# Decoding float64 weights beside an attention that TensorE bounds: the steps of a group gathered in one unit, a clamp on GpSimd, and the hash behind the values

## The chip, the core and the metric

The kernel runs on one core of a Trainium2 chip. The core has five engines that work side by side, each through its own queue in order: TensorE (PE; its weight loads are PEld), VectorE (DVE), ScalarE (ACT), GpSimd (POOL) and SyncE (SP), which here only issues transfers (DMA). The metric is device time in microseconds (us) of the whole program. Before the change it is 759.25 us, the median of three runs (758.73 to 759.68).

## The reference

Attention in which a query sees only the keys with the same six-bit hash, and behind it a feed-forward network with a convolution over the sequence and a gate. Four batches, 8 heads, 768 positions, head size 64; model width 512, inner width 1024, three taps.

```python
q_bits = (np.einsum('bhsd,dk->bhsk', q, proj) > 0).astype(np.int64)
k_bits = (np.einsum('bhsd,dk->bhsk', k, proj) > 0).astype(np.int64)
...
mask = q_bucket[:, :, :, None] == k_bucket[:, :, None, :]
scores = scale * np.matmul(q, k.transpose(0, 1, 3, 2))
scores = np.where(mask, scores, -1000000000.0)
scores = scores - np.max(scores, axis=-1, keepdims=True)
attn = np.exp(scores)
attn = attn / (np.sum(attn, axis=-1, keepdims=True) + 1e-09)
return np.matmul(attn, v).astype(np.float32)
...
h = np.maximum(x @ w_in, 0.0)
...
for k in range(K):
    conv_out += conv_w[k][None, None, :] * hp[:, k:k + S, :]
gate = 1.0 / (1.0 + np.exp(-conv_out))
return (h * gate @ w_out).astype(np.float32)
```

The weights w_in, w_out and conv_w come as float64.

## The kernel before

**Pairs and units.** Two heads of a batch form a pair: 16 pairs. A unit is 128 queries of one head of a pair; a pair has 12 units, in the order of its query blocks of 256 and, within a block, head 0 then head 1 with two units each. The outer loop runs over i = 0 to 194; k is the number of the unit within its pair (i = 12 x pair + k). Unit i issues: on TensorE its products (L253: four matmuls into one score buffer of PSUM, hash bits included as extra rows of K2 and Q2); on VectorE its maximum (L266), which also moves the scores to SBUF as tile e, and a small scaled copy of it (L270); the transposes of unit i - 3 (L296) on TensorE and their copy to SBUF, tile at (L303), on ScalarE; its exponential on ScalarE (L273). In the first six pairs the division by the sum is done behind the values: sums and their reciprocals (L287, L288) on VectorE, spread by GpSimd (rec, L290) and two transposes (L317); in the later pairs GpSimd divides e itself (L281).

**The values.** Every fourth unit (i = 7, 11, 15 and so on, AVS) issues the 24 matmuls of the values of one query block (L322). In the next unit ScalarE evicts (`high`: rs, L327, or xh, L336), and in the unit after that VectorE and GpSimd finish (`low`: x, L331, then xh and xl on GpSimd, L332 and L333, or xl, L339). [...]

**One ring of score buffers.** Scores, transposes and hashes take their PSUM tiles by turns from a ring of three ("S"). In program order products and transposes alternate, so each waits for the reader of the third before it: the transposes issued in unit i for VectorE's maximum of unit i - 1, and the products of unit i for ScalarE's copy of the transposes issued in unit i - 2. A hash takes a turn of its own.

**The next pair.** During a pair, `prepare` makes the operands of the next one out of its loaded Q and K (tile R, one buffer) in seven steps, one a unit: GpSimd rounds the high part (hi, L171), TensorE computes the hash (L186), VectorE makes bits of it (L189), GpSimd scales them (L191) and takes the low part (R, L176); SP sends every part to its rows (L174, L195, L178). It begins at k = 3 in the first pair, k = 2 in the second and k = 1 in the others (PREP). Six units later SP loads the next v and R (L165, L158); R's load must wait until the last low part (k<-R) has landed.

**The weights.** 16 blocks of 128 x 512 float64 numbers come as pairs of int32 words (rawi, rawo), one block loaded every four units (`fetch`, i = 2, 6, 10 and so on). A block takes nine steps: ScalarE's Abs of the upper word (L87, tile wl); VectorE's zero test (L89), shift and mask (L91), joining (L93), mask (L95) and lower part (L97); ScalarE's rounding (L105); GpSimd's subtraction and addition (L107, L109). `background` is called once a unit and moves each block that is under way on by a step (one or two instructions), each in another unit; a new block begins about every 4.1 units (RATE).

**The feed-forward** of a batch runs two pairs after its attention: 16 rounds of hidden (L360) and output (L390), with Relu, gate and taps on the other engines (L365 to L379). The first one stands behind unit 74.

The program order of each engine is the order in which this Python code issues; nothing reorders it.

Of the kernel before, what the change touches and what calls it, by code (L numbers as in the profile page):

```python
# [7 lines left out]
F32 = mybir.dt.float32  # L8
F32R = mybir.dt.float32r
# [24 lines left out]
AVS = (1 + NCK, 0, 0, 0)  # L34
PREP = (3, 2, 1)
PREP_N = 6
W0 = 6
RATE = 4.1
HRATE = 2.5
WC = 512  # L40
# [3 lines left out]
def lsh_attention_conv_ffn(ctx, tc, qk, v, hw, w_in, conv_w, w_out, consts, ident_in, out):  # L44
# [28 lines left out]

    def decode(raw, n, name):

        pr = raw.rearrange("p (n two) -> p n two", two=2)
        lo, hi = pr[:, :, 0].bitcast(U32), pr[:, :, 1].bitcast(F32)
        up, low = (ring(wp, bufs, [P, WC], I32, f"w{x}", f"w{x}{name}")[:, :n]
                   for x, bufs in (("u", 3), ("l", 3)))
        upf, lowf = up.bitcast(F32), low.bitcast(F32)
        V = nc.vector
        nc.scalar.activation(lowf, hi, AF.Abs)  # L87
        yield 2
        V.scalar_tensor_tensor(upf, lowf, F64_MIN, hi, ALU.is_ge, ALU.mult)  # L89
        yield 1  # L90
        V.tensor_scalar(low, up, 3, 0x3FFFFFFF, ALU.logical_shift_left, ALU.bitwise_and)  # L91
        yield 0
        V.scalar_tensor_tensor(up, up, -0x40000000, low, ALU.bitwise_and, ALU.bitwise_or)  # L93
        yield 2
        V.tensor_scalar(low, up, -0x800000, None, ALU.bitwise_and)  # L95
        yield 0
        V.scalar_tensor_tensor(lowf, lo, 2.0 ** -52, lowf, ALU.mult, ALU.mult)  # L97
        return upf, lowf

    def split_weight(raw, name):  # L100

        up, low = yield from decode(raw, WC, name)
        yield 2
        blk = weights[name] = cp.tile([P, 2, WC], F32R, tag=f"w{name}", name=f"w{name}")
        nc.scalar.copy(blk[:, 0, :], up)  # L105
        yield 2
        nc.gpsimd.tensor_tensor(up, up, blk[:, 0, :].bitcast(F32), ALU.subtract)  # L107
        yield 1
        nc.gpsimd.tensor_tensor(blk[:, 1, :], up, low, ALU.add)  # L109

    def decode_taps(raw):
        up, low = yield from decode(raw, NFC * 3, "cw")
        nc.vector.tensor_tensor(cw.rearrange("p f k -> p (f k)"), up, low, ALU.add)

# [13 lines left out]

    def background(rate, stop):

        step[0] += 1
        if rate and fetched and step[0] // rate > (step[0] - 1) // rate:
            splits.append(split_weight(*fetched.pop(0)))
        now = splits[:]
        while now:
            for g in now[:]:
                ended = next(g, None)
                if ended is None:
                    splits.remove(g)
                if ended is None or ended >= stop:  # L140
                    now.remove(g)

# [261 lines left out]
    def ffn(b, xs, fill, last):  # L404
# [4 lines left out]
        for i in range(len(todo) + FLAG):  # L409
            if i < len(todo):  # L410
                run.append(hidden(b, *todo[i], xs))
                next(run[i])
            if 1 <= i <= len(todo):
                next(run[i - 1], None)
            if i == 0:
                fill()
            fetch(1)
            background(HRATE, 2)
# [10 lines left out]
            background(HRATE, 2)  # L429

# [15 lines left out]
    for i in range(n + LAG):  # L446
# [15 lines left out]
        if u:
# [37 lines left out]
        if w and w.tq == QB // P - 1 and w.h == 1:  # L500
# [61 lines left out]
```

## Time and profile before

| | |
|---|---|
| Median of three runs | 759.25 us |
| Profiled execution: its own time | 758.92 us |
| Its span in the profile | 757.1 us |
| Granted TensorE clock | 0.99 |
| Attention with decode, feed-forward of batch 0 | to about 210, to about 282 us |

```profile
PE   5989989888889999999999999999999999999997
DVE  7778979778757646566657665666656665554653
...
PEclk8999999999999999999999999999999999999999
```

These lines cut the span in 40 slices of about 19 us and give the busy share of each in tenths. A row of the chain of waits has start, duration, engine and line; a row of a timeline has the tile that is written, the one read, and in brackets the idle time of the engine before it and what ended that. A row of groups has the count, the busy time in us and the mean of one in ns, then idle time. In the windows, each engine's busy time in us stands in the order PE, PEld, DVE, ACT, POOL, then clock, DMA share and GB/s.

### The profile page before, as it was taken

How to read it: one execution, taken by the hardware profiler on the slowest of the kernel's cores; microseconds unless marked ns; L12 is line 12 of the kernel's file. 1: busy time of each engine (PE TensorE's matmuls, PEld its weight loads, DVE VectorE, ACT ScalarE, POOL GpSimd, SP SyncE). 2: the span in 40 equal slices, each digit the busy share in tenths (PEclk: the TensorE clock that was granted, in tenths of full speed). 3: DMA queues.
4: the chain of work that ended last, by engine and by line, in shares of the span. 5: the costliest groups of instructions: out<-in, count | busy, mean ns of one | idle time of the engine just before them, and what ended most of it. 6: DMA issues, size and time to landing. Idle time of an engine off the chain costs nothing.

```text
span 757.1 us, 13345 instructions
## 1 busy us (share of the span) xinstructions
PE 717.0 (95%) x4588; PEld 586.6 (77%) x4588; DVE 498.0 (66%) x1212; ACT 511.9 (68%) x954; POOL 358.1 (47%) x355
## 2 busy tenths in 40 slices
PE   5989989888889999999999999999999999999997
PEld 3867767666679887777779988777779998778986
DVE  7778979778757646566657665666656665554653
ACT  5867777776755558778775547778775556875554
POOL 4345856565555324655735323556653433441222
PEclk8999999999999999999999999999999999999999
DMA  4656486482622103365541302256461211000011
GB/s 139 158 175 199 112 203 172 121 232 67 158 50 63 63 1 105 75 166 153 126 119 34 95 1 104 50 149 154 111 159 40 63 43 62 3 1 1 0 43 42
DMA packets 30355, 72.16 MB, mean 95 GB/s; under 512 B 5936, under 2 KB 7504, under 8 KB 30288
## 3 DMA queue, kind: packets, MB, share of 16 engines
q1 hardware_dynamic: 30000, 71.27, 34.8%
q8 instruction: 36, 0.59, 0.3%
q14 instruction: 31, 0.25, 0.1%
q10 hardware_dynamic: 288, 0.05, 0.0%
HBM read 27.40 MB, written 6.29 MB: 45 GB/s over the span
## 4 chain that ended last, share of the span: by engine, by line
PE 77%; DVE 15%; ACT 2%; DMA 2%; POOL 2%; issue 1%; DVEq 0%; SPq 0%; POOLq 0%; ACTq 0%
PE o L390 18%; PE h L360 17%; PE v L322 15%; PE s L253 13%; PE t L296 13%; DVE e L266 6%; DMA R<-in_qk 2%; PE hash L186 1%; DVE wuo L93 1%; DVE wlo L97 1%; DVE wui L93 1%; DVE st L270 1%; ACT e L273 1%; DVE wli L97 1%; DVE x L331 1%
## 5 line engine op out<-in xcount | busy, mean ns | idle before, releaser
L266 DVE TENSOR_SCALAR_CACHE_REDUCE e<-s 128x768 f32<-128x768 f32 x192 | 183.0, 953 | 87.3 <-PE s L253 80.8
L273 ACT ACTIVATE e<-e,st 128x768 f32<-128x768 f32 x192 | 180.7, 941 | 28.5 <-DVE st L270 13.9
L303 ACT COPY at<-t 128x768 f32<-128x768 f32 x192 | 152.0, 792 | 62.7 <-PE t L296 62.7
L296 PE MATMUL t<-ident,e 128*128 128x128 f32 x1152 | 162.6, 278 | 16.6 <-DVE e L266 14.0
L281 POOL TENSOR_SCALAR e<-e,st 128x768 f32<-128x768 f32 x120 | 109.2, 910 | 126.1 <-ACT at L303 65.0
L296 PEld LDWEIGHTS t<-ident,e 128*128 128x128 f32 x1152 | 130.9, 142 | 43.4 <-DVE e L266 23.7
L369 DVE SCALAR_TENSOR_TENSOR ht<-ht,cw 128x384 f32<-128x384 f32 (+1 forms) x128 | 113.1, 883 | 72.5 <-ACT ht L367 70.3
L379 POOL TENSOR_TENSOR g<-ht,g 128x384 fp32r<-128x384 f32 x64 | 72.9, 1138 | 169.3 <-ACT g L378 137.3
L390 PE MATMUL o<-wo,g 128*128 128x512 f32 x576 | 143.0, 394 | 1.0 <-POOL g L379 1.0
L360 PE MATMUL h<-xh,wi 128*128 128x386 f32 x512 | 142.2, 341 | 1.3 <-ACT ht L365 1.3
L322 PE MATMUL v<-at,v 128*64 128x256 f32 x1152 | 138.1, 385 | 0.0
L390 PEld LDWEIGHTS o<-wo,g 128*128 128x128 f32 x576 | 107.2, 188 | 22.0 <-POOL g L379 1.4
L253 PE MATMUL s<-K,Q 128*128 128x384 f32 x384 | 116.2, 384 | 3.9 <-DVE e L266 2.7
L322 PEld LDWEIGHTS v<-at,v 128*64 128x64 f32 x1152 | 83.2, 138 | 41.6 <-issue 9.2
L253 PE MATMUL s<-k,q 96*128 96x384 f32 x384 | 99.6, 340 | 2.5 <-DVE e L266 2.2
L360 PEld LDWEIGHTS h<-xh,wi 128*128 128x128 f32 x512 | 94.1, 188 | 5.3 <-ACT ht L365 1.8
L372 ACT ACTIVATE ht<-ht 128x384 f32<-128x384 f32 x64 | 33.6, 526 | 90.2 <-DVE ht L369 90.2
L360 PE MATMUL h<-xl,wi 128*128 128x386 f32 x256 | 86.8, 339 | 0.0
L253 PEld LDWEIGHTS s<-K,Q 128*128 128x128 f32 x384 | 58.5, 191 | 33.5 <-issue 18.6
L253 PEld LDWEIGHTS s<-k,q 96*128 96x128 f32 x384 | 70.6, 191 | 3.6 <-ACT q L233 3.1
L373 DVE TENSOR_TENSOR ht<-ht 128x384 f32<-128x384 f32 x64 | 43.1, 674 | 33.9 <-ACT ht L372 33.9
L176 POOL TENSOR_TENSOR R<-R,hi 128x768 fp32r<-128x768 f32 x30 | 59.2, 1973 | 0.2
(75 smaller groups left out, 613.5 us busy)
## 6 DMA issues: line engine op xcount, KB each, us to landing
R<-in_qk SPq DMA_DIRECT2D x15, 768.0 KB
K<-hi SPq DMA_DIRECT2D x60, 192.0 KB
v<-in_v SPq DMA_DIRECT2D x16, 384.0 KB
out<-osb SPq DMA_DIRECT2D x24, 256.0 KB
Q<-hi SPq DMA_DIRECT2D x30, 192.0 KB
q<-hi SPq DMA_DIRECT2D x30, 192.0 KB
Q<-R SPq DMA_DIRECT2D x30, 192.0 KB
k<-R SPq DMA_DIRECT2D x30, 192.0 KB
```

The source lines that it names most:

```text
L176: nc.gpsimd.tensor_tensor(lo, R, hi.bitcast(F32), ALU.subtract)
L253: nc.tensor.matmul(self.sp[:, half, :HS], A[:, h, qs], C[:, h, half * HS:(half + 1) * HS], start=(kk == 0), stop=(kk == 1))
L266: nc.vector.tensor_scalar(self.e.rearrange("p (a b) -> p a b", a=2), self.sp[:, :, :HS], MASKED, None, ALU.max, ALU.max, accum_out=self.st ...
L273: nc.scalar.activation(self.e, self.e, AF.Exp, bias=self.st[:, 1:2], scale=SCALE, accum_out=self.sum)
L281: nc.gpsimd.tensor_scalar(self.e, self.e, self.st[:, 3:4], 0.0, ALU.mult, ALU.add)
L296: nc.tensor.transpose(self.tp[:, c // 3, c % 3 * P:(c % 3 + 1) * P], self.e[:, c * P:(c + 1) * P], ident)
L303: nc.scalar.copy(pr.at[self.h][:, :, :, self.tq * P:(self.tq + 1) * P], self.tp[:, :, :3 * P].rearrange("p j (c q) -> p j c q", c=3))
L322: nc.tensor.matmul(av[h * D:(h + 1) * D, :QB], vt[:, c, h, :], ats[h][:, c // 3, c % 3, :], start=(c == 0), stop=(c == NCK - 1), tile_posi ...
L360: nc.tensor.matmul(hp[:, :HW], w, x[:, c0:c0 + HW], start=(n == 0), stop=(n == 3 * NCC - 1))
L369: nc.vector.scalar_tensor_tensor(t[:, a:z], ht[:, o + k - 1 + a:o + k - 1 + z], cw[:, f, k:k + 1], t[:, a:z], ALU.mult, ALU.add)
L379: nc.gpsimd.tensor_tensor(g[:, 1, :], t, g[:, 0, :].bitcast(F32), ALU.subtract)
L390: nc.tensor.matmul(op, l, r, start=(f == 0 and n == 0), stop=(f == NFC - 1 and n == 2))
```

## The change

- A block's decode is now `Decode`: `size` (ScalarE's Abs), `clamp` (GpSimd: minimum and maximum against two constants, in place), `upper` (VectorE: shift and mask of the clamped size, then joining with the raw upper word) and `lower` (VectorE, as before). The zero test L89 is gone: four VectorE steps instead of five.
- All blocks are one chain, `split_weights`. A block's size is issued one block ahead; its clamp is issued in the middle of the block before it, behind the subtraction and addition (`ends`) of the block before that.
- `background(3.75)` is called only in the units that issue values (`burst`, i = 7, 11 and so on) and issues three or four VectorE steps there, in front of the next unit's maximum; the feed-forward calls it twice a round with one step. The taps get their own generator, a step a unit.
- The values' `low` half waits for the next such unit; before, it came two units after the values.
- `prepare` begins at k = 3 in every pair: its hash stands directly behind the values' matmuls on TensorE, and each of its steps and transfers, with the loads of v and R, comes one or two units later than before from the second pair on.

The core of the diff:

```diff
-PREP = (3, 2, 1)
+PREP = 3
...
-W0 = 6
-RATE = 4.1
-HRATE = 2.5
+W0 = 7
+RATE = 3.75
...
+        def size(self):
+            nc.scalar.activation(self.lowf, self.hi.bitcast(F32), AF.Abs)
+        def clamp(self):
+            nc.gpsimd.tensor_scalar(self.lowf, self.lowf, F32_MAX, F64_MIN, ALU.min, ALU.max)
+        def upper(self):
+            V, up, low = nc.vector, self.up, self.low
+            V.tensor_scalar(low, low, 3, 0x3FFFFFFF, ALU.logical_shift_left, ALU.bitwise_and)
+            yield
+            V.scalar_tensor_tensor(up, self.hi, -0x40000000, low, ALU.bitwise_and, ALU.bitwise_or)
+            yield
...
+        while fetched:
+            raw, name = fetched.pop(0)
+            nxt = None
+            if fetched:
+                nxt = Decode(fetched[0][0], WC, fetched[0][1])
+                nxt.size()
+            yield from d.upper()
+            if ends:
+                ends()
+            if nxt:
+                nxt.clamp()
+            yield from d.lower()
+            blk = weights[name] = cp.tile([P, 2, WC], F32R, tag=f"w{name}", name=f"w{name}")
+            nc.scalar.copy(blk[:, 0, :], d.upf)
+            def ends(d=d, blk=blk):
+                nc.gpsimd.tensor_tensor(d.upf, d.upf, blk[:, 0, :].bitcast(F32), ALU.subtract)
+                nc.gpsimd.tensor_tensor(blk[:, 1, :], d.upf, d.lowf, ALU.add)
+            d = nxt
...
-    def background(rate, stop):
+    def background(n):
+        due[0] += n
+        while due[0] >= 1:
+            due[0] -= 1
+            next(weights_todo, None)
...
-        done, outs, lows = lows, [], outs
-        for high, low in lows:
+        burst = AVS[(i - LAG) % 4] > 0
+        for high, low in outs:
             high()
+        lows, outs = lows + outs, []
...
-        for high, low in done:
-            low()
+        if burst:
+            for high, low in lows:
+                low()
+            lows = []
...
+        if burst and i >= W0:
+            background(RATE)
-        if u and k == PREP[min(pi, 2)] and pi + 1 < len(pairs):
+        if u and k == PREP and pi + 1 < len(pairs):
             prep[0] = pairs[pi + 1].prepare()
```

VectorE's queue from the unit at i = 18 to the one at i = 20, before. The names carry batch, pair or chunk and a number; e and st belong to a unit (e_1_3_1 is pair 1, tile 3, head 1, i = 19, a values unit), wui and wli to a block of w_in.

```order
L270 TENSOR_SCALAR st_1_2_1_635<-st_1_2_1_635 128x1
L89 SCALAR_TENSOR_TENSOR wui_0_627<-wli_0_628,rawi_0_397 128x512
L266 TENSOR_SCALAR e_1_3_1_668,st_1_3_1_667<-s_1_3_1_662 128x768
L270 TENSOR_SCALAR st_1_3_1_667<-st_1_3_1_667 128x1
L91 TENSOR_SCALAR wli_0_628<-wui_0_627 128x512
L93 SCALAR_TENSOR_TENSOR wui_0_627<-wui_0_627,wli_0_628 128x512
L266 TENSOR_SCALAR e_1_4_0_707,st_1_4_0_705<-s_1_4_0_700 128x768
L270 TENSOR_SCALAR st_1_4_0_705<-st_1_4_0_705 128x1
L95 TENSOR_SCALAR wli_0_628<-wui_0_627 128x512
L97 SCALAR_TENSOR_TENSOR wli_0_628<-rawi_0_397,wli_0_628 128x512
```

And the same units after:

```order
L298 TENSOR_SCALAR st_1_2_1_636<-st_1_2_1_636 128x1
L294 TENSOR_SCALAR e_1_3_1_661,st_1_3_1_660<-s_1_3_1_655 128x768
L298 TENSOR_SCALAR st_1_3_1_660<-st_1_3_1_660 128x1
L359 TENSOR_TENSOR x_0_2_675<-v_0_2_512,rs_0_2_513 128x256
L96 SCALAR_TENSOR_TENSOR wui_0_446<-rawi_0_398,wli_0_447 128x512
L101 TENSOR_SCALAR wli_0_447<-wui_0_446 128x512
L103 SCALAR_TENSOR_TENSOR wli_0_447<-rawi_0_398,wli_0_447 128x512
L94 TENSOR_SCALAR wli_0_561<-wli_0_561 128x512
L294 TENSOR_SCALAR e_1_4_0_719,st_1_4_0_717<-s_1_4_0_712 128x768
```

x, three steps of one block and the first step of the next (wli_0_561) now all stand between the two maxima of i = 19 and i = 20.

GpSimd's queue at the same place, before (R_2 and hi_2 are the next pair's, xh and xl the finished values):

```order
L290 TENSOR_SCALAR rec_1_1_1_610<-sums_1_0_0_445 128x256
L332 TENSOR_SCALAR xh_0_277<-x_0_2_621 128x256
L333 TENSOR_TENSOR xl_0_278<-x_0_2_621,xh_0_277 128x256
L171 TENSOR_SCALAR hi_2_1_648<-R_2_372 128x768
L107 TENSOR_TENSOR wui_0_488<-wui_0_488,wi_0_625 128x512
L109 TENSOR_TENSOR wi_0_625<-wui_0_488,wli_0_489 128x512
```

and after:

```order
L318 TENSOR_SCALAR rec_1_1_1_617<-sums_1_0_0_457 128x256
L204 TENSOR_TENSOR R_2_375<-R_2_375,hi_2_0_564 128x768
L360 TENSOR_SCALAR xh_0_274<-x_0_2_675 128x256
L361 TENSOR_TENSOR xl_0_275<-x_0_2_675,xh_0_274 128x256
L133 TENSOR_TENSOR wui_0_316<-wui_0_316,wi_0_558 128x512
L134 TENSOR_TENSOR wi_0_558<-wui_0_316,wli_0_317 128x512
L89 TENSOR_SCALAR wli_0_561<-wli_0_561 128x512
L199 TENSOR_SCALAR hi_2_1_705<-R_2_375 128x768
```

The clamp of wli_0_561 (L89 of the changed kernel), on which VectorE's last step of the burst waits, stands behind xh, xl, subtraction and addition.

ScalarE's queue from i = 7 to i = 9, before (at is the copy of transposes, rs the values' factors):

```order
L273 ACTIVATE e_0_3_1_287,sums_0_2_0_204<-e_0_3_1_287,st_0_3_1_286 128x768
L327 COPY rs_0_0_280<-v_0_0_279 128x256
L303 COPY at_0_1_0_297<-t_0_3_0_332 128x6x128
L273 ACTIVATE e_0_4_0_329,sums_0_4_0_328<-e_0_4_0_329,st_0_4_0_327 128x768
L303 COPY at_0_1_1_298<-t_0_2_1_354 128x6x128
L273 ACTIVATE e_0_5_0_347,sums_0_4_0_328<-e_0_5_0_347,st_0_5_0_346 128x768
L87 ACTIVATE wli_0_377<-rawi_0_160 128x512
```

and after:

```order
L301 ACTIVATE e_0_3_1_284,sums_0_2_0_204<-e_0_3_1_284,st_0_3_1_283 128x768
L86 ACTIVATE wli_0_313<-rawi_0_160 128x512
L86 ACTIVATE wli_0_317<-rawi_0_272 128x512
L355 COPY rs_0_0_277<-v_0_0_276 128x256
L331 COPY at_0_1_0_294<-t_0_3_0_338 128x6x128
L301 ACTIVATE e_0_4_0_335,sums_0_4_0_334<-e_0_4_0_335,st_0_4_0_333 128x768
```

Two sizes now stand in front of the factors and of the copy, that of the first block (rawi_0_160) and that of the second (rawi_0_272). On SP the load of rawi_0_272 stands, before and after, fourteen transfers behind that of rawi_0_160: behind the first high part (four transfers), the bits (eight) and the first low part (two) of the next pair.

More of the change, by code (lines that the diff above doesn't have):

```diff
@@ L72, in lsh_attention_conv_ffn @@
     nc.vector.memset(zero[64:96], 0.0)
[L74 to L109, printed above, removed]
-    def decode_taps(raw):
-        up, low = yield from decode(raw, NFC * 3, "cw")
-        nc.vector.tensor_tensor(cw.rearrange("p f k -> p (f k)"), up, low, ALU.add)
+    class Decode:
+        def __init__(self, raw, n, name):
+            pr = raw.rearrange("p (n two) -> p n two", two=2)
+            self.lo, self.hi = pr[:, :, 0].bitcast(U32), pr[:, :, 1]
+            self.up, self.low = (ring(wp, 3, [P, WC], I32, f"w{x}", f"w{x}{name}")[:, :n] for x in "ul")
+            self.upf, self.lowf = self.up.bitcast(F32), self.low.bitcast(F32)
+        def size(self):
[8 more added lines that the diff above has]
+            yield
+        def lower(self):
+            V, up, low = nc.vector, self.up, self.low
+            V.tensor_scalar(low, up, -0x800000, None, ALU.bitwise_and)
+            yield
+            V.scalar_tensor_tensor(self.lowf, self.lo, 2.0 ** -52, self.lowf, ALU.mult, ALU.mult)
+            yield
@@ new lines, in split_weights @@
+    def split_weights():
+        d = Decode(fetched[0][0], WC, fetched[0][1])
+        d.size()
+        yield
+        d.clamp()
+        yield
+        ends = None
+        while fetched:
[16 more added lines that the diff above has]
+            d = nxt
+        ends()
@@ L116, in lsh_attention_conv_ffn @@
+    def decode_taps(raw):
+        d = Decode(raw, NFC * 3, "cw")
+        d.size()
+        yield
+        d.clamp()
+        yield
+        yield from d.upper()
+        yield from d.lower()
+        nc.vector.tensor_tensor(cw.rearrange("p f k -> p (f k)"), d.upf, d.lowf, ALU.add)
     blocks = [(w_in[c * P:(c + 1) * P, 2 * n * WC:2 * (n + 1) * WC], f"i{c}_{n}")
@@ L118, in lsh_attention_conv_ffn @@
     blocks += [(w_out[f * P:(f + 1) * P], f"o{f}") for f in range(NFC)]
-    fetched, splits, step = [], [], [0]
+    fetched, due, taps = [], [0], []
+    weights_todo = split_weights()
     def fetch(n):
@@ L127, in fetch @@
         del blocks[:n]
-    def background(rate, stop):
[L131 to L141, printed above, removed]
+    def background(n):
[3 more added lines that the diff above has]
+            next(weights_todo, None)
     class Pair:
@@ L477, in lsh_attention_conv_ffn @@
             next(first, None)
-        for high, low in done:
-            low()
+        if burst:
+            for high, low in lows:
+                low()
+            lows = []
         for _ in range(1 + NCK if ending else AVS[(i - LAG) % 4]):
@@ L494, in lsh_attention_conv_ffn @@
         if i == 3:
-            splits.append(decode_taps(cwr))
-        if i >= W0 - 4:
+            taps.append(decode_taps(cwr))
+        for g in taps:
+            next(g, None)
+        if i >= W0 - 5:
             fetch(i % 4 == 2)
-        if i >= 1:
-            background(RATE if i >= W0 else 0, 1)
         if w and w.tq == QB // P - 1 and w.h == 1:
```

11 lines of the change are left out of this document (5 added, 6 removed).

## The prediction

> **What bounds the kernel now.** First the page, then the stretches that it suggests.
>
> ```profile
> PE 717.0 (95%) x4588; PEld 586.6 (77%) x4588; DVE 498.0 (66%) x1212; ACT 511.9 (68%) x954; POOL 358.1 (47%) x355
> ...
> 48.09:190.12 142.03, 124.91 (x892) 96.66 (x894) 119.24 (x263) 105.78 (x193) 86.10 (x87) 0.99 0.59 158
> 291.66:380.69 89.03, 89.03 (x666) 68.73 (x668) 55.36 (x214) 70.03 (x131) 53.66 (x56) 1.00 0.47 117
> ```
>
> TensorE is busy for 95% of the span. The view of windows splits that: in the early stretch, where the weights are decoded, 124.9 of 142.0 us; in the late one, where attention stands alone, 89.0 of 89.0. Only early can this change win; late it can only lose. The chain of waits gives the length of a group of four units, from one values matmul to the next.
>
> ```profile
> 24.67 2.74 PE v L322 x24
> ...
> 48.09 3.07 PE v L322 x24
> ...
> 190.12 2.74 PE v L322 x24
> ...
> 291.66 2.76 PE v L322 x24
> 300.31 2.74 PE v L322 x24
> ...
> L317 PE MATMUL v<-ident,rec 128*128 128x128 f32 x36 | 7.4, 289 | 0.0
> ```
>
> Late, a group is 300.31 - 291.66 = 8.65 us, all TensorE. Early pairs add the transposes of the factors (7.4 us / 18 groups = 0.41): a floor of **9.05**, and 0.85 more in a group with a hash (row below). The values units are i = 7, 11, ..., 71; I call them V1 to V17. V1 starts at 24.67, V3 at 48.09, V16 at 190.12. Between V1 and V16 lie 15 groups, five with a hash: floor 15 x 9.05 + 5 x 0.85 = 140.0, measured 165.45, so **25.4 us over the floor**. The view of waits says where:
>
> ```profile
> PE t L296 <- DVE e L266: 14.0, 17, 1.4
> PE s L253 <- DVE e L266: 4.9, 5, 2.2
> PE hash L186 <- DMA R<-in_qk: 3.2, 2, 2.8
> PE hash L186 <- ACT wi L105: 3.0, 1, 3.0
> ```
>
> 18.9 us wait for VectorE's maxima, which stand in its queue behind decode steps; 6.2 us wait in front of a hash. (The last row names ScalarE; I take it for R's load as well, since a hash reads nothing that ScalarE's L105 writes.) Both kinds are what the change touches.
>
> **The change part by part.** *Removed.* One VectorE step per block, L89, goes:
>
> ```profile
> L89 DVE SCALAR_TENSOR_TENSOR wui<-wli,rawi x8: 695/1174/1618, 32.9 to 111.3; 128x512 f32<-128x512 f32 x8
> L97 DVE SCALAR_TENSOR_TENSOR wli<-rawi,wli x8: 692/693/693, 38.9 to 117.6; 128x512 f32<-128x512 uint32 x8
> L91 DVE TENSOR_SCALAR wlo<-wuo x8: 416/418/560, 123.8 to 205.6; 128x512 int32<-128x512 int32 x8
> ```
>
> That is 16 x about 1.2 us of VectorE time. The four that stay cost 0.42 (a shift or mask, L91) or 0.69 us (L97; L93 and the new form on the raw words are taken at the same) when nothing disturbs them: 2.2 us a block. The durations above those come from GpSimd:
>
> ```profile
> 47.30 1.27 POOL L109 TENSOR_TENSOR wi<-wui,wli 128x512 fp32r<-128x512 f32 x1
> ...
> 47.86 0.99 DVE L91 TENSOR_SCALAR wli<-wui 128x512 int32<-128x512 int32 x1
> ...
> 48.53 2.01 POOL L176 TENSOR_TENSOR R<-R,hi 128x768 fp32r<-128x768 f32 x1
> 48.89 2.20 DVE L93 SCALAR_TENSOR_TENSOR wui<-wui,wli 128x512 int32<-128x512 int32 x1
> ```
>
> L91 ends 0.28 after L109 does, L93 0.55 after L176: a decode step that meets a GpSimd step waits for its end and then runs; GpSimd's next step is held in turn (L176 began at 48.53, while L91 ran to 48.85). They alternate. For the place of a maximum:
>
> ```profile
> 51.09 0.62 PE L253 MATMUL s<-K,Q 128*128 128x384 f32 x2
> ...
> 52.10 0.96 DVE L266 TENSOR_SCALAR_CACHE_REDUCE e<-s 128x768 f32<-128x768 f32 x1 [1.01 <-PE s L253]
> ```
>
> *Moved: the burst.* All decode steps of a group (four, and three in every fourth group) now stand in the values unit between its maximum and the next. Let its products start at 0. A plain unit takes (8.65 - 2.74) / 4 = 1.48 on TensorE, half of it products. So after this unit (1.48), the factors (0.41), the values (2.74), the next unit (1.48) and products (0.74) it is at a transpose at 6.85, or 7.2 with values of 3.07 as at 48.09; I take 7.0. That transpose needs the score buffer that the next unit's maximum frees. VectorE begins the first maximum at 1.0 (51.09 to 52.10) and is through with it, its small step and x (some 0.45 together) at 2.4. From there it alternates with GpSimd's xh (0.41), xl (0.73), then subtraction and addition of an earlier block (1.27 for the addition above, and I take the subtraction at the same).
> - Four steps, clamp ready (V6 to V8, V10 to V12): 0.42 to 2.85, xh to 3.2, 0.69 to 3.8, xl to 4.5, 0.28 to 4.75, subtraction to 6.0, 0.55 to 6.55; the maximum ends at 7.55. TensorE waits **0.5**.
> - Three steps (V5, V9, V13), and V1, V2 with no earlier block: nothing.
> - The fourth kind (V3, V4, V14 to V17): a block's first step stands in the burst in which its clamp is issued, and that clamp stands on GpSimd behind xh, xl, subtraction and addition. Addition ends at 7.4, clamp 8.1, step 8.5, maximum 9.5: **2.5** each.
>
> *Added: the clamp.* No row shows it.
>
> ```profile
> L281 POOL TENSOR_SCALAR e<-e,st 128x768 f32<-128x768 f32 x120 | 109.2, 910 | 126.1 <-ACT at L303 65.0 <-DVE st L280 54.4 <-PE hash L186 3.8
> L332 POOL TENSOR_SCALAR xh<-x 128x256 fp32r<-128x256 f32 x18 | 8.3, 459 | 6.0 <-DVE x L331 6.0
> ```
>
> By columns between 256 (0.46) and 768 (0.91), 512 are **0.68**. Bounds: 0.46, and 1.27 (the two-input addition of as many): over six bursts -1.3 to +3.5 us. The Trainium skill, GPSIMD Engine Reference, "4.1 Engine selection", prefers VectorE for elementwise work but calls one-input steps on GpSimd roughly line-rate; by its 1.2 GHz 512 columns would be some 0.43 (an estimate), which would take 1.5 us from the sum. The rows show 768 in 0.91, slower than that, and I go by them.
>
> *Moved: ScalarE's first step.* The size (Abs) of the following block is now issued one block ahead, on ScalarE in front of the values' eviction and the next copy of transposes. In V1 to V4 that block's load was asked for only one unit earlier, and it stands on SP behind the next pair's Q and K transfers.
>
> ```profile
> 20.86 0.86 SPq L195 DMA_DIRECT2D k<-bits  x1
> ...
> 27.01 0.71 SPq L195 DMA_DIRECT2D q<-bits  x1
> ...
> 29.04 0.58 SPq L125 DMA_DIRECT2D rawi<-in_w_in  x1
> ...
> 30.08 0.59 PE L253 MATMUL s<-K,Q 128*128 128x384 f32 x2
> ...
> 35.84 0.60 SPq L178 DMA_DIRECT2D k<-R  x1
> ...
> 39.93 0.38 SPq L158 DMA_DIRECT2D R<-in_qk  x1
> 40.36 0.47 SPq L125 DMA_DIRECT2D rawi<-in_w_in  x1
> ...
> 42.21 0.66 ACT L87 ACTIVATE wli<-rawi 128x512 f32<-128x512 f32 x1
> ...
> 44.21 0.85 PE L186 MATMUL hash<-R,hw_sb 128*32 128x384 f32 x8 [2.79 <-DMA R<-in_qk]
> ...
> 45.21 0.62 DVE L189 TENSOR_SCALAR bits<-hash,cst 128x384 fp32r<-128x384 f32 x1 [2.88 <-DMA rawi<-in_w_in]
> ...
> 47.70 0.80 ACT L303 COPY at<-t 128x768 f32<-128x768 f32 x1 [3.22 <-PE t L296]
> ...
> 51.21 0.37 ACT L327 COPY rs<-v 128x256 f32<-128x256 f32 x1 [1.79 <-PE v L322]
> ```
>
> The load issued at 40.36 is the event nearest to 45.21: 4.85 us to land. The second block, issued at 29.04, would land at 33.9; then Abs 0.66, rs 0.37, the copy at 0.80: 35.7, and only then can TensorE run the products that started at 30.08. **V1 loses 5.6.** Its lost time hides the next one: the last part of K still lands some 4.1 after its issue (35.84 to 39.93), R follows, the third block lands at 44.4, ScalarE is through at 46.2 where the shifted schedule asks at 44.8: **1.4** more in V2. In exchange the wait for R at 44.21 falls inside. So V3 comes at about 49.5, 6.7 over the floor in two groups, where 48.09 is 5.3 over. V4 loses another **2.6**: its load stands on SP behind the pair's parts from V3. GpSimd has the first at 8.8 after V3's products (clamp and 0.8), four transfers of some 0.6 end at 11.2, the eight of the hash (20.86 to 27.72: 6.9) at 18.1, two more at 19.2; landed at 23.3 (4.1, no R ahead), ScalarE through at 25.1 (1.83), asked at 12.4 + 10.1 = 22.5. Later blocks are asked for five units or more ahead.
>
> *Moved: the hash* goes behind the values in all pairs. Its R has landed by then: the 6.2 us go, nothing else is late in their place there. But the pair's last K part now comes two units later (k = 9, not 7).
>
> ```profile
> 323.58 0.90 SPq L178 DMA_DIRECT2D k<-R  x1
> ...
> 327.78 0.39 SPq L158 DMA_DIRECT2D R<-in_qk  x1
> 333.58 0.61 PE L253 MATMUL s<-K,Q 128*128 128x384 f32 x2
> ```
>
> R's load is held until that part has landed, so 327.78 is its landing, 4.2 after issue; its first reader starts at 333.58, 0.85 sooner without the hash ahead of it. k = 7 to k = 9 takes a values unit and a plain one, 2.74 + 2 x (8.65 - 2.74) / 4 = 5.7. The margin of 5.8 shrinks to about nothing: I take 0.15 for each of some ten pairs, **+1.5**, with bounds of 0 and, at a landing of 5.2, 10.
>
> *x's step one values unit later*: it is in no one's way; its buffers have two groups.
>
> **Sum.** After, V1 to V16: 6.7 (V1, V2) + 2.5 x 4 (V3, V4, V14, V15) + 2.6 + 0.5 x 6 = 22.3 over the floor, before 25.4: -3.1. From V16 to the feed-forward: twice 2.5 = 5.0, and no decode is left in front of the last exponential; before, TensorE is idle there for 34.9 - 29.5 = 5.4 (row below): -0.4. K late: +1.5. Together **-2.0 us**, on the profiled 758.92 (span 757.1 and 1.8 around it), which lies 0.3 below the median of 759.25; on the median: **757.2**.
>
> ```profile
> 190.10:225.00 34.90, 29.50 (x205) 23.41 (x204) 24.23 (x50) 22.61 (x43) 19.44 (x20) 1.00 0.44 105
> ```
>
>
> **The rivals.**
> - *Faster.* The alternation is looser than I drew it: xl, subtraction and addition come when the burst is over, decode runs at 0.42 and 0.69, clamps end at about 6.8. Then the 0.5 vanish (-3.0) and each of the six 2.5 becomes 1.3 (-7.2): **747**. For it: half of L93's rows before are undisturbed. Against: there GpSimd had other units to work in. The Trainium skill, SBUF — State Buffer, "Who interferes with whom", has the port pair of VectorE and GpSimd locked for a whole instruction; the rows above agree, and by that rule this rival fails.
> - *No change.* K's last part lands late in every pair, 0.4 on average: +4 instead of +1.5: **759.7**. Early, a V4-like stretch gives it slack; late there is none.
> - *Slower.* ScalarE behind weights that have not landed. My price uses 4.85 from issue to landing. V8, V11 and V14 ask just as their block lands, by the chain hash, twelve transfers on SP, load. From about 5 us on, V1, V2, V4, V8, V11 and V14 each lose what is over; 6.5 us costs 6 x 1.65 = 10 us: **767**. For it: the load goes out amid Q and K transfers. Against: later, TensorE's own delays give ScalarE slack.
>
> **How the numbers follow.** Forecast 757.2, its own range 753 to 761, chance 0.42 (0.28 below 757.7, the rest within 0.2%, about 1.5 us, which is what a measurement can tell here, but for 0.02). Faster 0.20, no change 0.12 (half of it past 760.8), slower 0.26. Faster in all 0.48, same 0.18, slower 0.34. The range is 745 to 769: it takes in both outer rivals with the clamp's bounds on each side, and leaves out the K bound of 10 on top of a slow case.
>
> **What would show it.** The waits for VectorE's maxima fall only from 18.9 to about 18; the waits before a hash vanish; ScalarE stands idle some 5 us before the second Abs, near 28 us; in V3, V4 and V14 to V17 VectorE waits for GpSimd's clamp, elsewhere not; in the late stretch new waits of the products for K, each under 1 us. I am wrong if the decode in a burst runs undisturbed, or if the load of the second block lands before 29 us.

## The result, and the profile after

The changed kernel takes **776.35 us** (median of four runs, 774.61 to 778.0), the kernel before, beside it, 758.99 (758.38 to 759.68): a ratio of 1.0233, with a 95% interval of 1.0211 to 1.0254. The forecast was 757.2 in a range of 745 to 769. The profiled execution took 778.0, with a span of 775.6.

From the page of after, busy shares and the granted clock in 40 slices of 19.4 us:

```profile
PE 725.1 (93%) x4588; PEld 595.7 (77%) x4588; DVE 482.2 (62%) x1195; ACT 509.2 (66%) x954; POOL 365.5 (47%) x372
...
PE   5697988898699999999999999999999999999997
...
PEclk8898998999999999999999999999999999999999
```

TensorE is busier in us (725.1 against 717.0) for the same 4588 matmuls, and the clock row has four 8s among its first ten slices, where before had one, in the first. Both say that TensorE works slowly at times. The view of windows, from V1 to the first feed-forward and from there to the end, first before, then after (us; busy PE, PEld, DVE, ACT, POOL; clock; DMA):

```profile
24.60:210.21 185.61, 162.21 (x1159) 125.73 (x1159) 151.80 (x342) 137.31 (x251) 107.06 (x110) 0.98 0.59 158
210.21:757.14 546.93, 538.45 (x3345) 449.68 (x3343) 326.15 (x833) 358.13 (x677) 240.68 (x233) 1.00 0.27 72
```

```profile
24.65:226.57 201.92, 170.08 (x1151) 135.84 (x1151) 134.04 (x325) 134.66 (x250) 116.22 (x122) 0.89 0.53 146
226.57:775.60 549.03, 538.43 (x3353) 448.66 (x3351) 328.37 (x835) 358.23 (x679) 238.72 (x236) 1.00 0.27 72
```

16.3 us of the 18.5 are lost early, 2.1 late. VectorE did get lighter, by 15.8 us on the page (498.0 to 482.2), where the 16 zero tests had been put at 16 x 1.2. But TensorE has a clock of 0.89 early: (1 - 0.89) x 2 x 202 = 44 us at half speed. Before, 0.98 makes some 7. The view of TensorE's waits after:

```profile
PE t L324 <- DVE e L294: 11.7, 8, 3.4
PE s L281 <- DMA Q<-R: 9.8, 5, 4.4
PE s L281 <- ACT at L331: 7.3, 2, 5.4
PE s L281 <- DVE bits L217: 5.0, 2, 2.9
```

Many short waits (22 for VectorE's maxima before, 18.9 us) have become few long ones. The waits in front of a hash are gone, as expected; in their place stand the landing of Q's last part (9.8), a copy of ScalarE's (7.3) and the hash's bits (5.0). Where they fall, the starts of the values show:

```profile
80.71 2.81 PE L350 MATMUL v<-at,v 128*64 128x256 f32 x24
89.35 2.81 PE L350 MATMUL v<-at,v 128*64 128x256 f32 x24
```

V5 takes 89.35 - 80.71 = 8.64 us, without a wait: the true floor of an early group (9.49 with a hash, 0.85 more). The two transposes of the factors lie inside that; the prediction's 9.05 had added 0.41 for them to the late 8.65. Each group's length less this floor, from the starts of the values in the trace:

| group | before | foretold, over its 9.05 | after |
|---|---|---|---|
| V1 | 0.3 | 5.6 | 9.3 |
| V2 | 5.0 | 1.4 | 0.0 |
| V3 | 1.3 | 2.5 | 4.0 |
| V4 | 1.6 | 5.1 | 7.3 |
| V5, V6, V7 | 1.1, 1.6, 1.7 | 0, 0.5, 0.5 | 0.0, 0.4, 0.6 |
| V8 | 3.5 | 0.5 | 7.3 |
| V9, V10 | 1.0, 1.7 | 0, 0.5 | 0.0, 0.8 |
| V11 | 2.2 | 0.5 | 6.2 |
| V12, V13 | 2.3, 3.2 | 0.5, 0 | 0.1, 0.0 |
| V14, V15, V16 | 2.9, 2.3, 2.1 | 2.5 each | 5.4, 4.8, 5.2 |

So half of the groups run at the floor or nearly, better than before, and eight are 4 to 9 us over it. Three kinds, each from the timeline of after. **V1**, in which the second block's Abs stands on ScalarE in front of the copy that the products need:

```profile
28.52 0.59 SPq L160 DMA_DIRECT2D rawi<-in_w_in  x1
...
35.10 0.66 ACT L86 ACTIVATE wli<-rawi 128x512 f32<-128x512 f32 x1 [7.37 <-DMA rawi<-in_w_in]
...
35.91 0.80 ACT L331 COPY at<-t 128x768 f32<-128x768 f32 x1
...
36.77 1.01 PE L281 MATMUL s<-K,Q 128*128 128x384 f32 x2 [5.37 <-ACT at L331]
```

The load is issued at 28.52, landed at 35.10, and TensorE stands 5.4 us. **V16**, a burst of the fourth kind:

```profile
205.62 0.51 POOL L360 TENSOR_SCALAR xh<-x 128x256 fp32r<-128x256 f32 x1 [2.11 <-DVE x L359]
206.22 1.19 POOL L361 TENSOR_TENSOR xl<-x,xh 128x256 fp32r<-128x256 f32 x1
...
207.37 1.28 POOL L133 TENSOR_TENSOR wuo<-wuo,wo 128x512 f32<-128x512 f32 x1
...
208.73 1.28 POOL L134 TENSOR_TENSOR wo<-wuo,wlo 128x512 fp32r<-128x512 f32 x1
...
210.09 0.61 POOL L89 TENSOR_SCALAR wlo<-wlo 128x512 f32<-128x512 f32 x1
...
210.74 0.43 DVE L94 TENSOR_SCALAR wlo<-wlo 128x512 int32<-128x512 int32 x1 [3.91 <-POOL wlo L89]
...
212.31 0.94 DVE L294 TENSOR_SCALAR_CACHE_REDUCE e<-s 128x768 f32<-128x768 f32 x1
...
213.32 1.54 PE L324 MATMUL t<-ident,e 128*128 128x128 f32 x6 [3.44 <-DVE e L294]
```

Read downwards, it is the predicted chain on GpSimd, clamp behind xh, xl, subtraction and addition; VectorE's first step waits 3.9 us for it, TensorE 3.4 for the maximum behind that. And the transposes take 1.54 us, where six take 0.82 at full clock. In V3 and V15, which have a hash, the same late step delays the hash's bits on VectorE, and the products that need the hash's score buffer wait for those (5.0 in the view of waits). **V8**, where products wait for a part of the next pair's Q:

```profile
93.04 0.62 DVE L217 TENSOR_SCALAR bits<-hash,cst 128x384 fp32r<-128x384 f32 x1
94.12 1.28 POOL L134 TENSOR_TENSOR wi<-wui,wli 128x512 fp32r<-128x512 f32 x1
...
97.01 0.59 POOL L219 TENSOR_SCALAR bits<-bits,cst 128x384 fp32r<-128x384 f32 x1
...
99.56 0.79 SPq L223 DMA_DIRECT2D k<-bits  x1
...
105.14 0.71 SPq L223 DMA_DIRECT2D q<-bits  x1
...
107.16 0.59 SPq L160 DMA_DIRECT2D rawi<-in_w_in  x1
...
111.06 0.56 SPq L206 DMA_DIRECT2D Q<-R  x1
...
118.58 0.98 PE L281 MATMUL s<-K,Q 128*128 128x384 f32 x2 [4.40 <-DMA Q<-R]
...
119.07 0.39 SPq L186 DMA_DIRECT2D R<-in_qk  x1
```

The hash's bits are there at 93.66, but GpSimd scales them at 97.01, behind the burst's subtraction and addition. SP then issues eight small transfers (99.56 to 105.85), and behind them, within seven us, 2.4 MB of parts, v and weights. The last part of Q is issued at 111.06; what waits for the landing of both last parts, R's load, leaves at 119.07: 8.0 us later, or 7.4 from the issue of k's part at 111.66, the distance for which the prediction's late row had 4.2. The products would have started at 118.58 - 4.40 = 114.18, only 3.1 us after Q's part was issued.

### The profile page after: what moved, and what is told of

It reads as the page before. It is cut to its first block, busy times and chain, and to the rows that moved or that the text cites. A ratio compares the mean times of both kernels' runs of the same rounds, so it can differ in the third digit from the quotient of the medians.

```text
span 775.6 us, 13366 instructions
## 1 busy us (share of the span) xinstructions
PE 725.1 (93%) x4588; PEld 595.7 (77%) x4588; DVE 482.2 (62%) x1195; ACT 509.2 (66%) x954; POOL 365.5 (47%) x372
## 4 chain that ended last, share of the span: by engine, by line
PE 73%; DMA 8%; DVE 6%; POOL 5%; SPq 2%; issue 2%; ACT 2%; POOLq 0%; DVEq 0%; ACTq 0%
PE o L418 17%; PE h L388 17%; PE s L281 14%; PE t L324 12%; PE v L350 11%; DMA Q<-R 4%; DVE e L294 3%; DMA rawi<-in_w_in 1%; PE hash L214 1%; DMA k<-R 1%; ACT e L301 1%; DMA R<-in_qk 1%; SPq L223 1%; POOL wuo L133 1%; POOL xl L361 1%
## 5 line engine op out<-in xcount | busy, mean ns | idle before, releaser
L324 PE MATMUL t<-ident,e 128*128 128x128 f32 x1152 | 169.1, 286 | 12.9 <-DVE e L294 11.7
L324 PEld LDWEIGHTS t<-ident,e 128*128 128x128 f32 x1152 | 138.7, 147 | 34.1 <-DVE e L294 15.7
L397 DVE SCALAR_TENSOR_TENSOR ht<-ht,cw 128x384 f32<-128x384 f32 (+1 forms) x128 | 118.3, 925 | 72.9 <-ACT ht L395 69.7
L281 PE MATMUL s<-K,Q 128*128 128x384 f32 x384 | 120.9, 397 | 24.2 <-DMA Q<-R 9.8
L350 PE MATMUL v<-at,v 128*64 128x256 f32 x1152 | 135.1, 384 | 0.0
L350 PEld LDWEIGHTS v<-at,v 128*64 128x64 f32 x1152 | 78.6, 137 | 43.5 <-issue 8.9
L281 PE MATMUL s<-k,q 96*128 96x384 f32 x384 | 104.1, 353 | 3.0 <-DVE e L294 2.2
L281 PEld LDWEIGHTS s<-k,q 96*128 96x128 f32 x384 | 73.4, 200 | 6.2 <-ACT q L261 3.1
L401 DVE TENSOR_TENSOR ht<-ht 128x384 f32<-128x384 f32 x64 | 36.2, 566 | 33.0 <-ACT ht L400 33.0
L204 POOL TENSOR_TENSOR R<-R,hi 128x768 fp32r<-128x768 f32 x30 | 55.2, 1839 | 0.0
```

The source lines that it names most:

```text
L204: nc.gpsimd.tensor_tensor(lo, R, hi.bitcast(F32), ALU.subtract)
L281: nc.tensor.matmul(self.sp[:, half, :HS], A[:, h, qs], C[:, h, half * HS:(half + 1) * HS], start=(kk == 0), stop=(kk == 1))
L324: nc.tensor.transpose(self.tp[:, c // 3, c % 3 * P:(c % 3 + 1) * P], self.e[:, c * P:(c + 1) * P], ident)
L350: nc.tensor.matmul(av[h * D:(h + 1) * D, :QB], vt[:, c, h, :], ats[h][:, c // 3, c % 3, :], start=(c == 0), stop=(c == NCK - 1), tile_posi ...
L397: nc.vector.scalar_tensor_tensor(t[:, a:z], ht[:, o + k - 1 + a:o + k - 1 + z], cw[:, f, k:k + 1], t[:, a:z], ALU.mult, ALU.add)
```

## The experiments

All times are medians in us; the ratio is to the kernel before on the same chip, with its 95% interval. "Over" is a group's length less 8.64 (9.49 with a hash). Unless said otherwise a kernel is the changed one with the edit shown.

### One block's load earlier

```diff
-            fetch(i % 4 == 2)
+            fetch((i % 4 == 2) + (i == 2))
```

> The changed kernel with two weight blocks loaded at i = 2 instead of one, so that every later block is asked for one group (four units) earlier. Theory A (ScalarE stands behind a load that hasn't landed): the 5.4 us in V1 and the 2.0 in V4 go with their half-clock windows (2.6 and about 1): -10 to -11, 766; the waits for K's parts may move, since the load comes at another time. Rival (V1's loss only hides that of V2 and V3, which come back): -4, 772.

**765.58**, ratio 1.0085 (1.0051 to 1.0118): 10.8 less than the changed kernel. V1 falls from 9.3 over to 1.0, V4 from 7.3 to 4.3. As theory A said: the wait behind an unlanded load was dear, and its loss did not hide another's.

### The clamp ahead of the subtraction

```diff
+            if nxt:
+                nxt.clamp()
             if ends:
                 ends()
-            if nxt:
-                nxt.clamp()
```

> The changed kernel with the clamp of the following block issued on GpSimd ahead of the subtraction and addition of an earlier block instead of behind them. Theory C (VectorE's first decode step stands behind a clamp that stands behind both): the clamp is through 2.6 us earlier in V3, V4 and V14 to V16, the five stalls there (2.4, 2.9, 3.1, 3.1, 3.6) shrink to about 0.5 to 1, too short for a half-clock window, so 2.4 and 1.7 fewer each: about -18, 758. Rival (it is the sharing of the port, not the order: the same steps alternate with VectorE anyway): within 3 us of 776.

**774.24**, ratio 1.0200 (1.0161 to 1.0240). A miss. Where theory C could be seen alone it held in part: V3 4.0 to 1.8, V15 4.8 to 2.1, V16 5.2 to 4.1, V14 5.4 to 5.2. But V4 rose from 7.3 to 12.3, an 8.4 us wait behind its unlanded load: TensorE came there earlier, the load did not.

### A whole block in each burst

```diff
-RATE = 3.75
+RATE = 4
...
-            background(RATE)
+            background(2 if i == W0 else RATE)
```

> The changed kernel with the steps dealt so that every burst decodes exactly one block: two steps in V1 (size and clamp of the first block), then four in each of V2 to V17. No first step stands in the burst in which its clamp is issued, and the second block's Abs moves from V1 to V2. Theory A + C: V1's 9.3 over the floor fall to about 1, those of V3, V4 and V14 to V16 (4.0, 7.3, 5.4, 4.8, 5.2) to 0.5 to 1 each; V8 and V11 (7.3, 6.2), which wait for K's and Q's parts, stay: 776.4 - 8.3 - 23 = 745. Rival (the four steps against subtraction and addition cost the same wherever they stand, and a waiting ScalarE moves to another place): 765 to 776.

**753.99**, ratio 0.9947 (0.9927 to 0.9966): half a per cent faster than the kernel before, 22.4 less than the changed one, by two numbers that only decide which step falls in which burst. V1 is at 0.0 over, V3 0.6, V4 0.3, V15 0.1, V16 1.0: the clamp's and the load's stalls are gone. It misses its 745, since the wait for Q's last part now stands at V5 too (7.7), beside V8 (6.9), V11 (7.0), and V14 (5.2): at two places an earlier loss had hidden it.

### The hash: put back, and moved alone

The changed kernel with the old PREP:

```diff
-PREP = 3
+PREP = (3, 2, 1)
```

> The changed kernel with the hash step alone put back to where it stood (k = 3, 2, 1). Theory K (the last part of K and Q lands late because the parts were moved two units back): the waits of the products for that part, 4.4 us at 118.6, 3.0 at 152.4 and some 2 in the late stretch, vanish, and with the first two the half-clock windows behind them (2.6 us each): about -14, so 762; should the waits of a hash for R come back (6.2 before), up to 768. Theory of the prediction (the hash in its old place costs 6.2, the parts cost 1.5): 776.4 + 6.2 - 1.5 = 781.

**774.53**, ratio 1.0205 (1.0165 to 1.0245). The parts behave as theory K says: V8 7.3 to 3.9 over (1.8 of it a wait for R), V11 6.2 to 1.1, late stretch 549.0 to 545.5. But V4 and V15 rise by 1.9 and 2.7, and V6, V7, V9, V10, V12 by 0.8 to 1.7 each: with k = 1 another step of `prepare`, R's low part (1.84 us on GpSimd), stands in the bursts. The net says nothing about either theory; the groups do.

The kernel before with the new PREP:

```diff
-PREP = (3, 2, 1)
+PREP = (3, 3, 3)
```

> The kernel before with the hash behind the values (k = 3 in all pairs) and nothing else. Prediction: the two waits in front of a hash (6.2) go, late parts cost 1.5: 754.3. Theory K: the parts land late where a weight's load shares the DMA engines with them, two places of 3 to 4.4 us and 2.6 of half clock behind each, and 2 in the late stretch, against 6.2 gained: 759 + 9 = 768.

**761.18**, ratio 1.0028 (1.0011 to 1.0044). From V1 to the feed-forward 185.6, as before. Its TensorE waits:

```profile
PE t L296 <- DVE e L266: 22.6, 27, 1.6
...
PE s L253 <- DVE e L266: 2.3, 2, 1.8
```

The 6.2 us in front of a hash are gone and the waits for VectorE's maxima, 18.9 before, are 24.9: the hash was late because TensorE was early, and VectorE takes over. Late it costs 2.1 (546.9 to 549.0). Neither theory had this; there is no wait for Q's parts early, and none of SP's weight loads goes out within 6 us ahead of a last part, so the hash's place alone does not make V8's and V11's.

### The hash one unit earlier, ahead of the decode steps

```diff
-PREP = 3
+PREP = 2
...
-        if burst and i >= W0:
-            background(RATE)
         if u and k == PREP and pi + 1 < len(pairs):
             prep[0] = pairs[pi + 1].prepare()
         next(prep[0], None)
+        if burst and i >= W0:
+            background(RATE)
```

> The changed kernel with the hash one unit earlier (k = 2, the unit ahead of the values) and its steps issued ahead of the decode steps of the same unit, in VectorE's and GpSimd's queues. Theory K (the bits' scaling stands on GpSimd behind subtraction, addition and clamp, so the eight transfers and all that SP issues behind them go out some 5 us later and meet a weight's load): the waits for Q's and K's parts in V8 and V11 go with their half clock (7.3 and 6.2 over the floor become 1), the late ones too (2): 776.4 - 12.5 - 2 = 762. Rival (it is the load beside the parts alone): V8 and V11 keep 5 or more, above 770.

**788.42**, ratio 1.0412 (1.0369 to 1.0454). V8 and V11 fall to 0.5 and 0.4 over, as theory K has it. The total is worse: V3, V15 and V16 rise to 6.2, 7.0 and 7.5, where R's low part on GpSimd (1.80 us in V16) meets the late first decode step on VectorE (2.02 us there, where 0.43 was seen above); V1 begins 3.5 later (the second pair's hash, ahead of V1, waits 2.7 for R), and the late stretch grows to 559.0 (waits of 1 us for GpSimd's rows). The same with whole blocks, so that no decode step is late:

> Both: whole blocks in each burst, and the hash one unit earlier and ahead of the decode steps. If both theories hold, the sum of both: 745 - 14 = 731, and 27 us below the kernel before. If a stall that one of them removes only hid the other's, 740 to 750.

**752.26**, ratio 0.9931 (0.9904 to 0.9958). No half-clock window is left between V1 and the feed-forward, which take 165.1 against 185.6 before. What misses 731 is the 3.5 at the start, the late stretch of 557.3, and some 1 us over in most groups.

### Are the weights' loads what makes the parts late?

Three edits of the kernel with whole blocks. All loads two units earlier: `fetch(i == 2 or i % 4 == 0)`.

> The kernel with whole blocks in each burst, and with the weight loads after the first issued at i = 4, 8, 12, ... instead of i = 6, 10, 14, ...: on SP they then stand ahead of the hash's eight small transfers and not between the parts of K and Q. Theory L (the last parts land 7 us after their issue, not 4.2, since 0.5 MB of weights share the DMA engines with them): V5, V8, V11 and V14 fall from about 7 over the floor to 2 or less, since the stall of 2.6 to 4.5 shrinks below the 1.7 that takes the clock: 754 - 4 x 5 = 734. Rival (the parts are late because GpSimd scales the hash's bits late, and SP issues everything behind that): they keep 5 or more each, 750 to 755.

**758.49**, ratio 0.9993 (0.9967 to 1.0019). Inconclusive: SP, some 6 us behind with the hash's transfers, issued the loads among the parts nonetheless. So did it when V8's and V14's loads were moved by one group, `fetch({30: 2, 34: 0, 54: 2, 58: 0}.get(i, i % 4 == 2))`:

> The kernel with whole blocks in each burst, and at two of its four late places, V8 and V14, no weight load: those of i = 34 and 58 are issued together with the ones of i = 30 and 54. V5 and V11 are left as they are, for comparison within the run. (Moving all loads by two units did not clear the place, since SP was some 6 us behind and issued them among the parts anyway.) Theory L (the load beside the parts makes the landing 7 us instead of 4.2): V8 and V14 fall from 6.9 and 5.2 over the floor to 2 or less, V5 and V11 keep about 7: 754 - 8 = 746. Rival (the parts are issued late, behind the hash's transfers and GpSimd's bursts, load or not): V8 and V14 keep 5 or more, 754.

**757.15**, ratio 0.9969 (0.9947 to 0.9991), but with two loads at V8 and V14 now, and there 8.3 and 7.6 over instead of 6.9 and 5.2. Further away, `fetch({26: 3, 30: 0, 34: 0, 50: 3, 54: 0, 58: 0}.get(i, i % 4 == 2))`:

> Whole blocks in each burst, and now no weight load among the parts at V8 and V14: those of i = 30 and 34 are issued with the one of i = 26, those of 54 and 58 with the one of 50, which SP reaches long before. V5 and V11 keep one load each. With two loads (the last run's V8 and V14) the last part of K landed 9.5 and 8.7 us after that of Q was issued, with one 6.7 to 7.9, so with none 5.5 to 6 by the trend: theory L, then, gives a stall of about 2 less at V8 and V14 and, if it falls under 1.7, no half-clock window: over the floor 1 to 3 instead of 7 and 5; 754 - 7 = 747. Rival (the clump alone: all parts leave SP behind the hash's eight transfers, whatever else is loaded): V8 and V14 stay above 4.5, 751 or more.

**745.01**, ratio 0.9819 (0.9756 to 0.9882). V8's rows of SP, from the timeline of the kernel with two loads and then of the one with none:

```profile
91.86 0.58 SPq L160 DMA_DIRECT2D rawi<-in_w_in  x1
92.49 0.45 SPq L160 DMA_DIRECT2D rawo<-in_w_out  x1
...
96.09 1.09 SPq L206 DMA_DIRECT2D Q<-R  x1
...
105.55 0.39 SPq L186 DMA_DIRECT2D R<-in_qk  x1
```

```profile
96.73 0.54 SPq L206 DMA_DIRECT2D Q<-R  x1
...
103.00 0.39 SPq L186 DMA_DIRECT2D R<-in_qk  x1
```

From the issue of Q's last part to that of R's load: 9.5 us with two loads (8.7 at V14), 6.7 to 7.9 with one, 6.3 with none (5.7 at V14). In the kernel before with the hash moved alone it is 3.6 to 4.3 early. V8 and V14 fall to 3.7 and 2.2 over, V5 (one load, 7.0 to land) keeps 6.1. V11, which was left alone, falls from 7.0 to 3.4 as well, since its stall of 3.2 happens to straddle two of the clock's stretches (last section) and costs no half clock; so 6 of the 9 us gained are the loads'. A load adds some 1.5 us to the landing, then, which leaves some 2 for the clump of parts behind the hash's transfers; that share is a difference, not measured by itself. Moving the hash takes the clump apart: with the hash one unit earlier the distance was 3.6 us in V7, for the products of V8, though a load had gone out 3.8 us ahead of the part, but 7.0 in V13, where a load had gone out 0.7 us ahead of it.

### TensorE's clock

```diff
+    FILL_S = {10: 24, 17: 8, 22: 6, 38: 18, 50: 12, 65: 12}
+    FILL_T = {21: 10, 61: 12, 69: 14}
...
+            for _ in range(count):
+                nc.tensor.matmul(idle[:, :HS], pr.Q1[:, 0, :P], pr.K1[:, 0, :HS], start=True, stop=True)
```

> The changed kernel with idle TensorE filled: in front of the nine stalled instructions (units 10, 17, 21, 22, 38, 50, 61, 65, 69) stand 6 to 24 further products whose result nobody reads, about as long as the stall less 0.5 to 1 us. All waits stay as they are. Theory D (a stall of more than 1.7 us in one of the clock's stretches of 3.4 us sends TensorE to half speed in the next, and that costs 13.9 of the 17 us): the half-clock windows of V1, V3, V4, V8, V11 and V14 to V16 vanish and with them 10 to 14 us: 763 to 766. Rival (the lost clock only fills time that the next wait would take anyway): within 3 us of 776.

**775.25**, ratio 1.0233 (1.0197 to 1.0269): 1.1 less than the changed kernel, within the spread of its four runs (772.86 to 777.46). Six of the eight groups have no half-clock stretch any more and are 1.4 to 2.7 us shorter each: V1 9.3 to 7.4, V3 4.0 to 2.4, V8 7.3 to 4.6, V11 6.2 to 4.8, V15 and V16 4.8 and 5.2 to 3.2 and 3.6, 10.8 in all. 9.9 come back, in V2 (1.7), V4 (4.6), V14 (1.8) and V17 (1.8, up to the feed-forward). Its waits of TensorE say for whom: in V2 and V4 for ScalarE behind a load (1.0 and 5.1), in V14 for Q's part (2.3), in V17 for the maximum behind a late clamp (1.8).

```profile
PE s L281 <- ACT at L331: 7.8, 3, 5.1
PE s L281 <- DMA Q<-R: 6.7, 5, 2.3
PE t L324 <- DVE e L294: 6.5, 9, 1.8
```

A rest of a stall stays behind each filling, so it did not cost time itself. V4, V14 and V17 have half-clock stretches still, 13.7 us of them where the changed kernel has 44.4. Theory D falls as a sum: 31 us of half clock went and 1.1 us of time with them; most of what the clock took, the next wait would have taken.

### A version that beats both

Whole blocks, the hash ahead of the decode steps, and its unit by stretch:

```diff
-PREP = 3
+PREP = (3, 2, 2, 2, 2, 2, 1)
...
-        if u and k == PREP and pi + 1 < len(pairs):
+        if u and k == PREP[min(pi, 6)] and pi + 1 < len(pairs):
```

> Whole blocks in each burst, with the hash at k = 3 in the first pair, at k = 2 ahead of the decode steps in the next five, and at k = 1 in the late stretch. The kernel with k = 2 everywhere lost 3.5 us in the first pair (V1 at 28.16 instead of 24.65) and 10 us late (waits of the transposes for GpSimd's normalised rows, 1 us each). If both come from the unit of the hash alone: 752.3 - 3.5 - 10 = 739. Rival (the first pair's loss only moves the wait for its hash to V2, and the late waits come from the burst): 748 to 752.

**742.39**, ratio 0.9777 (0.9732 to 0.9822): nearer to the sum than to the rival. The late stretch is 543.3; but V2 is 5.5 over, its hash waits 2.9 for R. With k = 2 in the first pair as well:

> As the kernel with k = 3 in the first pair, 2 in the next five and 1 late (742.4), but with k = 2 in the first pair too. V1 then starts 3.4 us later (28.16 instead of 24.75), but the second pair's hash, which waited 2.9 us for R in V2 with a half-clock window behind it (5.5 over the floor), waits 0.6 (0.8 over): 742.4 + 3.4 - 4.7 - 2 (other hashes' waits for R) = 739. Rival (R is late for the second pair by the unit of its own hash alone): 745 to 746.

**738.55**, ratio 0.9748 (0.9723 to 0.9772), 20 us below the kernel before. From its timeline, a burst:

```profile
185.87 0.61 DVE L94 TENSOR_SCALAR wlo<-wlo 128x512 int32<-128x512 int32 x1
186.52 0.69 DVE L96 SCALAR_TENSOR_TENSOR wuo<-rawo,wlo 128x512 int32<-128x512 int32 x1
...
187.25 0.43 DVE L101 TENSOR_SCALAR wlo<-wuo 128x512 int32<-128x512 int32 x1
187.71 0.69 DVE L103 SCALAR_TENSOR_TENSOR wlo<-rawo,wlo 128x512 f32<-128x512 uint32 x1
187.89 1.66 POOL L133 TENSOR_TENSOR wuo<-wuo,wo 128x512 f32<-128x512 f32 x1 [1.69 <-ACT wo L130]
```

No first step waits for a clamp: in this burst, V17's, the four follow each other in 2.5 us, and the subtraction starts during the last of them.

## Why the prediction was wrong

- **The floor** was 0.41 too high a group: the transposes of the factors are inside the 8.64. Over the 15 groups to V16 that hid 6.2 us of before's losses; with the true floor the forecast would have been lower by as much, and further off.
- **V1: mechanism right, size too small.** The load took 6.6 us from issue to Abs (28.52 to 35.10), not 4.85, and its landing at 35.1 instead of 33.9 stalled TensorE 5.4 us; the half clock behind it brought the term of 5.6 to 9.3. V2's 1.4 was hidden. One load earlier gave 10.8 back, 8.3 of it in V1, so this step is shown.
- **The bursts.** Four steps with a ready clamp were foretold at 0.5; V6, V7, V10 and V12 have 0.1 to 0.8: right. The clamp takes 0.61 (0.68 foretold). The fourth kind was foretold at 2.5 in six bursts; V3, V14, V15 and V16 have 4.0 to 5.4: the chain is the predicted one, its stall 2.1 to 3.4 and the half clock behind it the rest. ScalarE's Abs of a later block also waits there for the addition (three buffers), which the text had not seen; it comes free with the clamp, and did not decide. Dealing whole blocks took the stalls away: shown. V17, the sixth of the kind, has three steps, of which the last waits 1.9 us for its clamp; TensorE waits 0.9 for the maximum behind it. Up to the feed-forward V17 is 1.5 us shorter than before, but 0.85 of that is the hash that stood there.
- **K's last part is the step that failed.** The text said "I take 0.15 for each of some ten pairs" and that early "a V4-like stretch gives it slack". Both the 4.2 us of landing and the 5.8 of margin came from the late stretch. Early, the bits' scaling moves behind the burst's steps on GpSimd, SP's eight transfers with it, and everything that SP holds back then goes out at once beside a weight's load: from k's issue to R's load 7.4 us at V8 and 6.7 at V11, with 3.1 and 3.9 us from the issue of Q's part to the place of its reader. With the half clock, V8 and V11 lose 13.5 us over the floor, where the sum had 0.5 each. The long landing was there to be read. From SP's queue in the kernel before, in V7:

```profile
93.99 0.60 SPq L125 DMA_DIRECT2D rawi<-in_w_in  x1
...
95.20 0.59 SPq L178 DMA_DIRECT2D k<-R  x1
...
103.92 0.39 SPq L158 DMA_DIRECT2D R<-in_qk  x1
```

That is 8.7 us from k's issue; in V10, V13 and V16 it is 5.4, 6.5 and 5.5, in V2 and V4 4.1 and 3.9. Before the change it reached TensorE only through R, for which the prediction took the hash at 108.44 to wait; in V7, V10, V13 and V16 the parts' own readers came more than 10 us after their issue. Late, where neither burst nor load exists, the term of 1.5 came out at 2.1. That is partly luck: landing took 3.9 to 5.8 us there, not 4.2, and the text had put the cost at 10 for 5.2.
- **The hash's 6.2** went, but, as the hash alone shows, into VectorE's maxima, not into time.
- **The clock** was in no term. Taking two thirds of the half clock away was worth about 1 us of the total, but without the clock the sizes at the single places can't be understood.
- **The tally.** By the table, V1 to V15 are 23.6 us over what was foretold: 12.5 in V8 and V11, 5.2 in V14 and V15, 3.7 in V3 and V4, 2.3 in V1 and V2 (the sum itself went by 6.7 for these two, not 5.6 + 1.4); the too high floor takes 6.2 of it back.
- **The rivals.** Slower was given 0.26, at 767, with ScalarE behind unlanded weights as its mechanism. That is 10.8 of the loss; V8 and V11, where it too saw trouble, lost to Q's part instead. The tight alternation of VectorE and GpSimd held: the looser case (747) did not come.

## What to carry to other kernels

Gathering an engine's work in one place makes it regular only if everything that the first step needs was issued a whole burst earlier: count, for each burst, which steps are fed from within it. A landing time read in a quiet stretch (4.2 us here) does not hold where other transfers leave the same queue together (up to 8.7 in the same trace); read it, or its bound, in the stretch in which it will be used. And when a stall is removed, look for the transfer that runs on its own time behind it: in three of these runs a repaired place gave part of its gain to a later one.

## What the runs showed of the hardware

TensorE's clock answers to idleness in fixed stretches. The view of windows, two neighbouring stretches of after and two of before (length, then busy PE; the clock is third from the end):

```profile
56.20:59.61 3.41, 1.30 (x8) 0.87 (x7) 2.02 (x5) 1.63 (x3) 2.80 (x4) 1.00 0.00 0
59.61:63.02 3.41, 3.41 (x17) 3.31 (x15) 2.30 (x7) 2.75 (x5) 1.76 (x2) 0.50 0.95 225
```

```profile
106.75:110.16 3.41, 1.72 (x14) 1.09 (x15) 1.23 (x5) 2.13 (x4) 2.37 (x5) 1.00 0.63 256
110.16:113.58 3.42, 3.42 (x31) 2.87 (x31) 3.28 (x8) 2.42 (x4) 3.42 (x3) 1.00 0.80 191
```

Every half-clock stretch is 3.41 us or a multiple of it (but for those at a program's end), and within a run all start on one grid of 3.41. Over all fifteen traces, without the first 18 and the last 6 us, 54 stretches of that grid at full clock were followed by half clock: TensorE was busy in them for at most 1.84 us. 3078 were not: at least 1.73 (the stretch from 106.75 above, whose edges are rounded there). The bound is thus about half a stretch, 1.7 to 1.8 us. The Trainium skill, TensorE: Matmul & The Clock Gate, "Part 1: The HAM clock gate", describes such free-running windows of 3.413 us, with which the trace agrees; the rule of the same page under "Why this matters for your kernels", no idle gaps above about 3 us, is too mild here: the stall of 2.1 us at 58.5 was enough.
